# Pair loads from the fifth chunk on, the last ten gate products on VectorE, and a new order in a scan and mixture-of-adapters kernel

## The chip, the cores and the metric

The kernel runs on one core of a Trainium2 chip. A core has five engines with queues of their own: TensorE (PE in the profile; PEld is its loading of weights), VectorE (DVE), ScalarE (ACT), GpSimd (POOL) and SyncE (SP), which here only issues DMAs. The metric is the device time of one execution in microseconds (us), the median of three runs. The profile shows one execution, whose instructions span a little less than its time.

## The reference

Two steps. The first is a linear recurrence along 6400 positions for each of 8 sequences and 128 features; the second sends every row of the result (51200 rows of 128) through two of eight low-rank adapters.

```
h = a[:, t] * h + b[:, t];  x[:, t] = h            # t = 0 .. 6399
logits = x @ w_gate                                # 8 experts
topk = the two largest logits of a row
w = softmax over these two
out = x + sum over the two experts e of w[e] * (x @ A[e]) @ B[e]     # A: 8 x 128 x 16, B: 8 x 16 x 128
```

All arrays are float32. a and b are 26.2 MB each, and so is the output.

## The kernel before, in words

**Tiles.** The 51200 rows are 100 chunks of 512 rows (256 KB of a, of b and of the output). A chunk counts as four blocks of 128 rows. Six blocks make a unit (the last four units have four blocks), four units a group (the last six groups have 2, 2, 1, 1, 1 and 1 units).

**One chunk's way.** SyncE loads a and b (`load`, line 526; the DMA itself is line 541). TensorE transposes them to features by rows (line 562: a to pA, b to pB). ScalarE copies pA to a_st (line 580), VectorE scans (line 613, reading a_st and pB, writing xT in float16; a chunk that holds the border of a sequence is scanned in two pieces). For a unit TensorE multiplies xT with all adapters' A and the gate (line 633, to pZ), and ScalarE copies the result to zl (line 639). For a group the gating (lines 667 to 688) finds the best two experts and their weights g: two maxima and the last product on VectorE, a sigmoid on ScalarE, and the wide steps between on GpSimd, for the last six groups on VectorE instead. Then, again by chunks (`back`, line 693): the gate product zw = zl * g (line 707 on GpSimd, line 711 on VectorE), TensorE transposes zw (line 720), the transposed block is copied to zwT (line 729 on VectorE, line 726 on ScalarE), TensorE adds x and zwT times B in one accumulator (lines 734 and 735), ScalarE copies it to outt (line 744), and SyncE stores it (line 779).

**Loads.** In before the first 8 chunks (HEAD) are loaded singly, 256 KB a DMA, a row of four consecutive rows (2 KB) to each partition, and transposed in four 128-row transposes for a and four for b. From chunk 8 on `paired(c)` (line 523) is true: two chunks come in one DMA of 512 KB, eight consecutive rows (4 KB) to each partition, so that the first chunk of the pair lies in partitions 0 to 63 and the second in 64 to 127. Each takes eight 64-row transposes for a and eight for b. `front` (line 582) interleaves a transpose group of b of chunk c with one of a of chunk c + 1, so that the upper and the lower half of the array work together (line 597): such a group needs the load of b of chunk c and that of a of chunk c + 1, and a step of it feeds the copy of one chunk and the scan of another. Six pairs of buffers hold the loads (12 chunks); a load waits until the transposes of the chunk before it in that buffer are done. Output buffers hold 18 chunks. Stores go in pairs too, except those of the last four chunks.

**Which engine in the tail.** MU_DVE (line 117) lists the chunks, counted from the end, whose gate product is on VectorE: in before 1, 2, 4, 6 and 8, that is chunks 99, 98, 96, 94 and 92. TE_LAST (line 114) lists those of the last 12 chunks whose zwT copy is on ScalarE: none. SPLIT (line 126) sends the stores that begin at chunks 56 and 78 as two DMAs, of 120 and 8 partitions.

**The order.** The program is written as a list of steps, each with an engine, an assumed duration and the steps that it depends on. Before anything runs a planner (`schedule`, line 208) fixes the order on every engine: each step has a rank, its place in a period of six chunks plus TEMPLATE plus NUDGE (line 28), and of the steps whose rank lies within WINDOW of the first in the engine's queue the one that can start earliest goes next. The planner's loads and stores have assumed rates (LOAD_RATE, STORE_RATE, PAIR_RATE). On the chip the engines run these orders and wait for one another by semaphores. `la12` is the load of a that begins at chunk 12, `lb` that of b, `sc` the scan, `A`, `B` and `P` transposes, `te` the zwT copy, `mu` and `md` the gate product on GpSimd and on VectorE.

Of the kernel before, what the change touches and what calls it, by code (L numbers as in the profile page):

```python
# [15 lines left out]
PE_FREE = 0.1  # L16
Q_RATE = {3: 3.6e-3, 5: 2.1e-3, 7: 2.1e-3}
SCAN_SELF = 0.13
ISSUE = {"sp": 0.52, "act": 0.45}
LOAD_RATE = 392e3  # L20
STORE_RATE = 408e3
# [86 lines left out]
START = (-999, "", 0)  # L108
FIRST = -9999
EARLY = -400  # L110
LEAD = []
TAPER = [2, 2, 1, 1, 1, 1]
WIDE_DVE = [1, 2, 3, 4, 5, 6]
TE_LAST = []
TAIL_UNITS = [4, 4, 4, 4]
TE_ACT = [1]
MU_DVE = [1, 2, 4, 6, 8]
TAIL_CHUNKS = 12
WARM0 = 12
WARM = 16  # L120
HALVES = 0.745
PAIR_RATE = 411e3
HEAD = 8
TAIL = 0
STORE_TAIL = [1, 1, 1, 1]
# [754 lines left out]
```

## Time and profile before

| | |
|---|---|
| median of 3 runs | 207.19 us (206.95 to 208.16) |
| the profiled execution | 207.91 us |
| its span, first to last instruction | 205.9 us |
| TensorE clock, mean granted | 0.975 |
| busy: PE, PEld, DVE, ACT, POOL | 184.7, 160.9, 177.7, 169.1, 144.6 us |
| moved by DMA | 79.26 MB, 385 GB/s over the span |
| HBM read, written | 52.56 MB, 26.21 MB |
| VectorE scans (line 613) | 92 whole ones, 1275 ns each |
| gate products on GpSimd (line 707), on VectorE (line 711) | 95 of 1069 ns, 5 of 682 ns |

In the page the span is cut into 40 equal slices; a digit is the busy share of a slice in tenths, PEclk is the clock granted to TensorE, GB/s what the DMA engines moved. In the stretches each engine has its busy microseconds and, in brackets, its instructions, in the order PE, PEld, DVE, ACT, POOL. In a timeline a bracket at the end of a row gives the idle time before it and what ended that. The chain of waits is followed back from the last instruction; its rows are the start and the length of each piece.

### The profile page before, as it was taken

The page shows a single profiled execution, that of the slowest core. Times are in us where ns is not written, and L with a number is a line of the kernel's source. Part 1 is how long each engine was busy: PE and PEld are TensorE (multiplying, and loading weights), DVE is VectorE, ACT ScalarE, POOL GpSimd, SP SyncE. Part 2 cuts the span into 40 slices and gives each one's busy share as a digit, 9 for nine tenths or more (in the row PEclk, how much of TensorE's full clock was granted, in tenths as well). Part 3 has the DMA queues.
Part 4 walks back from the last instruction along what each step waited for, and adds up shares of the span by engine and source line. Part 5 has one row for each costly group of instructions (what it writes and reads, how often), then busy time and mean ns, then how long its engine had stood idle before and what let it go on. Part 6 is the DMA issues. An engine that isn't in the chain of part 4 may idle for free.

```text
span 205.9 us, 7539 instructions
## 1 busy us (share of the span) xinstructions
PE 184.7 (90%) x3152; PEld 160.9 (78%) x3152; DVE 177.7 (86%) x289; ACT 169.1 (82%) x306; POOL 144.6 (70%) x176
## 2 busy tenths in 40 slices
PE   7779589999998899899799999999999999879683
PEld 6557478887897789788689888988888888857572
DVE  0789688998998899798899999999997999989881
ACT  2356668999998999899799999999999998886372
POOL 1000328879898978878788988899989898687420
PEclk9999958999999999999999999999999999999789
DMA  6999999999999999999999999999999999997388
GB/s 191 368 392 415 405 409 406 405 409 405 411 417 406 414 403 417 409 403 416 408 409 400 409 395 408 415 410 411 409 412 410 410 409 404 405 352 289 132 299 300
DMA packets 30559, 79.26 MB, mean 385 GB/s; under 512 B 3774, under 2 KB 3902, under 8 KB 30526
## 3 DMA queue, kind: packets, MB, share of 16 engines
q1 hardware_dynamic: 29054, 78.39, 97.1%
q10 hardware_dynamic: 1472, 0.40, 0.8%
q8 instruction: 25, 0.41, 0.8%
q14 instruction: 8, 0.07, 0.1%
HBM read 52.56 MB, written 26.21 MB: 383 GB/s over the span
## 4 chain that ended last, share of the span: by engine, by line
PE 67%; DVE 12%; DMA 10%; POOL 3%; issue 3%; SPq 2%; ACT 1%; DVEq 0%; POOLq 0%
PE pA L562 14%; PE pB L562 12%; PE pZ L633 11%; PE pO L734 10%; PE pO L720 10%; PE pO L735 9%; DMA a_tm<-in_a_dram 7%; DVE xT L613 5%; DMA b_tm<-in_b_dram 3%; POOL zw L707 3%; SPq L541 2%; DVE zwT L729 2%; DVE zw L711 1%; ACT outt L744 1%; DVE g L688 1%
## 5 line engine op out<-in xcount | busy, mean ns | idle before, releaser
L613 DVE TENSOR_TENSOR_SCAN xT<-a_st,xT,pB 128x512 f16<-128x512 f32 x96 | 120.3, 1253 | 9.5 <-PE pA L562 5.6
L707 POOL TENSOR_TENSOR zw<-zl,g 128x512 f16<-128x512 f32 x95 | 100.4, 1069 | 24.7 <-PE pO L720 11.3
L562 PE MATMUL pB<-ident_f,b_tm 64*128 64x64 f32 (+1 forms) x768 | 71.4, 235 | 6.5 <-DMA a_tm<-in_a_dram 2.8
L580 ACT COPY a_st<-pA 128x512 f32<-128x512 f32 x100 | 60.5, 612 | 17.5 <-PE pA L562 16.0
L562 PE MATMUL pA<-ident_f,a_tm 64*128 64x64 f32 (+1 forms) x768 | 71.7, 235 | 2.0 <-DMA a_tm<-in_a_dram 1.0
L562 PEld LDWEIGHTS pB<-ident_f,b_tm 64*128 64x128 f32 (+1 forms) x768 | 57.9, 142 | 12.5 <-issue 3.7
L562 PEld LDWEIGHTS pA<-ident_f,a_tm 64*128 64x128 f32 (+1 forms) x768 | 57.9, 142 | 8.2 <-DMA a_tm<-in_a_dram 2.3
L639 ACT COPY zl<-pZ 128x816 f32<-128x816 f32 (+1 forms) x68 | 58.0, 853 | 2.3 <-PE pZ L633 1.6
L744 ACT COPY outt<-pO 128x512 f32<-128x512 f32 x92 | 52.7, 609 | 7.7 <-PE pO L735 7.3
L734 PE MATMUL pO<-ident_h,xT 128*128 128x128 f16 x368 | 50.1, 223 | 1.2 <-DVE zwT L729 1.0
L735 PE MATMUL pO<-cst_h,zwT 128*128 128x128 f16 x368 | 48.9, 220 | 0.8 <-issue 0.8
L734 PEld LDWEIGHTS pO<-ident_h,xT 128*128 128x128 f16 x368 | 40.5, 114 | 4.8 <-DVE zwT L729 2.1
L633 PE MATMUL pZ<-cst_h,xT 128*128 128x136 f16 x400 | 36.5, 228 | 1.5 <-DVE xT L613 0.6
L735 PEld LDWEIGHTS pO<-cst_h,zwT 128*128 128x128 f16 x368 | 36.9, 100 | 0.8 <-issue 0.8
L720 PE MATMUL pO<-ident_h,zw 128*128 128x128 f16 x368 | 33.2, 221 | 2.0 <-ACT outt L744 1.3
L729 DVE COPY zwT<-pO 128x512 f16<-128x512 f16 x77 | 30.2, 410 | 3.4 <-PE pO L720 3.1
L633 PEld LDWEIGHTS pZ<-cst_h,xT 128*128 128x128 f16 x400 | 27.1, 115 | 4.4 <-DVE xT L613 1.3
L720 PEld LDWEIGHTS pO<-ident_h,zw 128*128 128x128 f16 x368 | 22.3, 98 | 6.0 <-issue 1.9
L669 POOL TENSOR_TENSOR k<-zl,m 128x192 f32<-128x192 f32 x15 | 7.8, 519 | 22.9 <-DVE m L667 22.9
L671 POOL TENSOR_SCALAR L<-k 128x192 f32<-128x192 f32 x15 | 12.9, 860 | 1.3
L613 DVE TENSOR_TENSOR_SCAN xT<-a_st,pB 128x512 f16<-128x512 f32 (+1 forms) x8 | 7.5, 939 | 4.6 <-PE pB L562 4.3
L678 POOL TENSOR_TENSOR L<-k,m 128x192 f32<-128x192 f32 x15 | 7.9, 524 | 2.8 <-DVE m L676 2.7
(41 smaller groups left out, 106.1 us busy)
## 6 DMA issues: line engine op xcount, KB each, us to landing
a_tm<-in_a_dram SPq DMA_DIRECT2D x46, 512.0 KB, 10.7
b_tm<-in_b_dram SPq DMA_DIRECT2D x46, 512.0 KB, 10.6
out_dram<-outt SPq DMA_DIRECT2D x46, 512.0 KB, 10.8
a_tm<-in_a_dram SPq DMA_DIRECT2D x8, 256.0 KB, 5.8
b_tm<-in_b_dram SPq DMA_DIRECT2D x7, 256.0 KB, 6.0
out_dram<-outt SPq DMA_DIRECT2D x4, 256.0 KB, 2.7
out_dram<-outt SPq DMA_DIRECT2D x2, 480.0 KB
b_tm<-in_b_dram ACTq DMA_DIRECT2D x1, 256.0 KB, 3.6
```

The source lines that it names most:

```text
L562: last = eng["pe"].transpose(*args)
L580: lambda: eng["act"].copy(a_st[c % NA][:, :], pA[:, c % 2, :]), fr(c, "ae"))
L613: last = eng["dve"].tensor_tensor_scan(out=x[:, s0:s1], data0=a_st[c % NA][:, s0:s1], data1=pB[:, c % 2, s0:s1], initial=init, op0=ALU.mul ...
L633: last = eng["pe"].matmul(pZ[:, k // (n // 2), o : o + W], xblock(b0 + k), Awg_h)
L639: return eng["act"].copy(zl[:, zb : zb + n, :].rearrange("p (h k) w -> p h (k w)", h=2), pZ[:, :, 0 : n // 2 * W])
L671: lambda e: e.tensor_scalar(out=ll, in0=kk, scalar1=0.0, scalar2=-1.0e30, op0=ALU.is_ge, op1=ALU.mult), dve=not main)
L707: lambda: eng["pool"].tensor_tensor(out=wv, in0=zv, in1=gv, op=ALU.mult), ba(gi, c, "mu"))
L720: last = eng["pe"].transpose(ptile[:, k * 128 : k * 128 + 128], zw[w][:, k, :], ident_h[:, :])
L729: lambda: eng["dve"].tensor_copy(zwT[w][:, :], ptile[:, 0:C]), ba(gi, c, "te"))
L734: eng["pe"].matmul(dst, xblock(b0 + k), ident_h[:, :], start=True, stop=False)
L735: last = eng["pe"].matmul(dst, zwT[w][:, k * 128 : k * 128 + 128], B_h, start=False, stop=True)
L744: lambda: eng["act"].copy(outt[:, o0 : o0 + n, :].rearrange("p k w -> p (k w)"), bank),
```

## The change

HEAD goes from 8 to 4, so chunks 0 to 3 are loaded singly. FLAT names the pairs 2 to 5, that is chunks 4 to 11: these are loaded two at a time, but in the layout of the single loads (2 KB rows) and with 128-row transposes, and their transposes of a and b are groups of their own. From chunk 12 on everything is as before. MU_DVE takes in all of the last ten chunks, and TE_LAST the zwT copies of chunks 99, 98, 96, 94, 92 and 90. SPLIT is empty. The planner gets two margins (2 us ahead of steps of SyncE, 1 us behind a load), other rates and windows, and new ranks throughout. HEAD_UNITS is empty, so what it touches stays as it was, and the edit to the dependencies of `T` says the same in other words.

```diff
+SP_MARGIN = 2.0
+LAND_MARGIN = 1.0
-LOAD_RATE = 392e3
-STORE_RATE = 408e3
+LOAD_RATE = 387e3
+STORE_RATE = 413e3
 NUDGE = {
...
-    -28.418, "g1_20": 31.602, "g2_15": -5.737, "g2_16": -48.614, "g2_17": -1.558, "g2_18": -9.806, "g2_19": 25.794,
...
+    "A1": 0.12, "A12": -0.295, "A5": -2.998, "B0": 0.543, "B10": 0.408, "B4": -0.719, "B5": -0.252, "B9": 0.072,
...
-WINDOW = {'pe': 16.262, 'act': 17.153, 'dve': 47.02, 'pool': 47.064, 'sp': 57.831}
+WINDOW = {'pe': 8.807, 'act': 27.754, 'dve': 12.829, 'pool': 5.533, 'sp': 45.819}
-TE_LAST = []
+TE_LAST = [1, 2, 4, 6, 8, 10]
+HEAD_UNITS = []
+FLAT = [2, 3, 4, 5]
-MU_DVE = [1, 2, 4, 6, 8]
+MU_DVE = [1, 2, 3, 4, 5, 6, 7, 8, 9, 10]
-PAIR_RATE = 411e3
-HEAD = 8
+PAIR_RATE = 414.5e3
+HEAD = 4
-SPLIT = {56: [120, 8], 78: [120, 8]}
+SPLIT = {}
 TEMPLATE = {
-    "la": [-13.284, -13.376, -10.147],
-    "lb": [-12.856, -11.393, -13.112],
-    "A": [3.619, 4.619, -4.264, 6.619, 7.619, 8.619],
-    "B": [-2.245, 2.718, -8.407, 8.99, 6.061, 4.41],
+    "la": [-6.553, -4.617, -2.553],
+    "lb": [-6.553, -4.553, -2.553],
+    "A": [0.912, 2.517, 3.517, 4.517, -3.092, 9.66],
+    "B": [-0.301, 3.648, 4.517, 1.944, 6.315, 7.517],
...
+    def margin(self, d, op):
+        return (SP_MARGIN if op.eng == "sp" else 0.0) + (LAND_MARGIN if d.sem is not None else 0.0)
...
-                users[d.i].append((op, self.lag(d, op)))
+                users[d.i].append((op, self.lag(d, op) + self.margin(d, op)))
...
         def paired(c):
-            return HEAD <= c < NCH - TAIL
+            return HEAD <= c < NCH - TAIL and c // HC not in FLAT
...
-                    q, f"{key}{c}", n * C * D * 4 / (PAIR_RATE if paired(c) else LOAD_RATE),
+                    q, f"{key}{c}", n * C * D * 4 / (PAIR_RATE if paired(c) else STORE_RATE if n == HC else LOAD_RATE),
```

More of the change, by code (lines that the diff above doesn't have):

```diff
@@ L121 @@
 HALVES = 0.745
-PAIR_RATE = 411e3
-HEAD = 8
+PAIR_RATE = 414.5e3
+HEAD = 4
 TAIL = 0
 STORE_TAIL = [1, 1, 1, 1]
-SPLIT = {56: [120, 8], 78: [120, 8]}
+SPLIT = {}
 TEMPLATE = {
-    "la": [-13.284, -13.376, -10.147],
-    "lb": [-12.856, -11.393, -13.112],
-    "A": [3.619, 4.619, -4.264, 6.619, 7.619, 8.619],
-    "B": [-2.245, 2.718, -8.407, 8.99, 6.061, 4.41],
-    "ae": [-1.493, 12.357, 10.831, 7.96, 5.931, 11.772],
-    "sc": [-2.149, -1.286, 6.521, -19.69, -9.638, -0.216],
-    "Z": [6.623, 2.916, -2.696, 9.959],
-    "ze": [6.413, 12.686, 18.636, 4.611],
-    "g1": [1.078],
-    "g2": [15.192],
-    "g3": [12.311],
-    "g4": [-7.624],
-    "g5": [43.586],
-    "g6": [18.91],
-    "w1": [27.261],
+    "la": [-6.553, -4.617, -2.553],
+    "lb": [-6.553, -4.553, -2.553],
+    "A": [0.912, 2.517, 3.517, 4.517, -3.092, 9.66],
+    "B": [-0.301, 3.648, 4.517, 1.944, 6.315, 7.517],
+    "ae": [-6.291, 2.578, 3.093, 6.695, 6.06, 7.06],
+    "sc": [-1.377, -1.34, 1.899, 2.384, 4.614, 4.743],
+    "Z": [-1.773, 4.921, 1.502, 2.727],
+    "ze": [-4.588, 0.759, -5.543, 3.442],
+    "g1": [3.016],
+    "g2": [4.586],
+    "g3": [3.551],
+    "g4": [2.992],
+    "g5": [3.066],
+    "g6": [1.968],
+    "w1": [3.121],
     "w2": [27.183],
@@ L146 @@
     "p3": [35.473],
-    "mu": [22.377, 11.789, 38.051, -6.995, 25.901, 25.822],
-    "T": [17.564, 18.694, 15.643, 19.013, 20.568, 20.925],
-    "te": [11.47, 21.167, 12.791, -1.785, 1.996, 11.732],
-    "D": [13.525, 17.402, 15.169, 14.035, 19.652, 27.901],
-    "oe": [26.926, 32.894, 33.316, 36.556, 35.829, 26.06],
-    "st": [25.679, 26.621, 29.881],
-    "ta": [14.725, 30.746, 16.943, 18.052, 19.161, 20.27],
-    "md": [78.718, -0.018, -87.87, 12.1, 13.209, 14.318],
+    "mu": [11.649, 11.861, 13.38, 13.442, 14.624, 15.545],
+    "T": [11.704, 10.769, 11.92, 12.841, 15.097, 14.896],
+    "te": [11.106, 11.632, 13.124, 14.809, 14.966, 15.856],
+    "D": [10.274, 11.213, 12.116, 13.037, 15.506, 24.201],
+    "oe": [2.576, 7.213, 7.951, 8.765, 12.054, 10.102],
+    "st": [27.605, 29.678, 31.678],
+    "ta": [-10.83, 12.148, -0.969, 14.045, 14.966, 15.887],
+    "md": [10.94, 11.861, 13.636, 13.703, 14.624, 15.545],
     "wu": [-0.198],
-    "ch": [26.813],
+    "ch": [2.449],
     "mb": [0.0],
-    "q2": [17.668],
-    "q3": [-16.399],
-    "q5": [-0.842],
-    "q6": [-2.93],
-    "q7": [1.928],
+    "q2": [4.085],
+    "q3": [3.453],
+    "q5": [3.066],
+    "q6": [3.093],
+    "q7": [3.107],
     "q8": [35.473],
-    "g7": [47.426],
-    "g8": [9.111],
+    "g7": [3.107],
+    "g8": [3.132],
 }
@@ L348, in bass_associative_scan_2x2__then__mixture_of_adapters_kernel @@
     b0 = 0
-    for n in [U] * ((NBLK - sum(TAIL_UNITS)) // U) + TAIL_UNITS:
+    for n in HEAD_UNITS + [U] * ((NBLK - sum(HEAD_UNITS) - sum(TAIL_UNITS)) // U) + TAIL_UNITS:
         units.append((b0, n))
@@ L513, in un @@
         def un(u, kind):
-            return (PERIOD * (u // GMAX), kind, u % GMAX)
+            v = u - len(HEAD_UNITS)
+            if v < 0:
+                return ((units[u][0] + units[u][1] - 1) // J - 1, kind, 0)
+            return (sum(HEAD_UNITS) // J + PERIOD * (v // GMAX), kind, v % GMAX)
         def ga(gi, kind):
@@ L721, in tr @@
                 return last
-            o_T[c] = P.add("pe", f"T{c}", 0.1 + 0.056 * n, [(o_mu[c], True), (o_ih, True)] + free + [(o, True) for o in o_wu if c < 2], tr, ba(gi, c, "T"))
+            o_T[c] = P.add("pe", f"T{c}", 0.1 + 0.056 * n, [(o_mu[c], True), (o_ih, True)] + free + [(o, True) for o in (o_wu if c < 2 else [])], tr, ba(gi, c, "T"))
             if te_act(c):
```

95 rows, old and new, of the table NUDGE are left out of this document.

## The prediction

> **What bounds the kernel now.** I read the slices first, then busy time by stretches, then the chain of waits and the timelines of the first 30 and the last 25 us. The page's span and slices:
>
> ```profile
> span 205.9 us, 7539 instructions
> ...
> PEclk9999958999999999999999999999999999999789
> DMA  6999999999999999999999999999999999997388
> GB/s 191 368 392 415 405 409 406 405 409 405 411 417 406 414 403 417 409 403 416 408 409 400 409 395 408 415 410 411 409 412 410 410 409 404 405 352 289 132 299 300
> DMA packets 30559, 79.26 MB, mean 385 GB/s; under 512 B 3774, under 2 KB 3902, under 8 KB 30526
> ```
>
> A slice is 205.9 / 40 = 5.15 us. From the third to the 35th the DMA engines are full at about 409 GB/s; only the first two slices and the last five fall short. The bytes do not change, so time can be won only where they are short: 79.26 MB at 409 GB/s is 193.8 us, and the other 12.1 us lie at the ends. Busy time by stretches (engine, busy us, count; then granted clock, DMA share, GB/s):
>
> ```profile
> 0.00:10.00 10.00, 7.28 (x40) 6.11 (x41) 3.56 (x5) 3.25 (x5) 0.70 (x6) 1.00 0.84 276
> ...
> 24.00:40.00 16.00, 15.12 (x256) 13.02 (x256) 13.64 (x18) 13.07 (x22) 10.92 (x14) 0.79 1.03 409
> 40.00:180.00 140.00, 134.14 (x2508) 118.63 (x2504) 130.43 (x198) 130.04 (x236) 121.29 (x146) 1.00 1.03 409
> 180.00:206.00 26.00, 17.98 (x238) 15.01 (x235) 18.87 (x62) 14.47 (x31) 11.09 (x10) 0.93 0.74 274
> ```
>
> The first 10 us move 2.76 MB where 409 GB/s would give 4.09: 3.3 us lost. The last 26 us run at 274: (409 - 274) / 409 x 26 = 8.6 us lost. That is the 12 us. In the last stretch only stores are left and they wait for results: the compute chain, with VectorE (third pair of numbers) its fullest engine, sets the end. In the body VectorE is busy 130.43 of 140 us. Who waits for whom, SyncE's queue and then VectorE in the body (40 to 175 us):
>
> ```profile
> SPq L541 <- PE pA L562: 40.9, 25, 4.5
> ```
> ```profile
> DVE xT L613 <- PE pA L562: 3.8, 8, 1.1
> ```
>
> Loads wait 40.9 us for TensorE to free their buffers, so in the body compute is behind the loads. An idle microsecond saved on VectorE anywhere is a microsecond off the end, until the DMA floor: 193.8 + 3.3 + 2.2 for the last store (the final output copy of the chain below ends at 203.05; 205.9 - 203.05 = 2.85, of which 256 KB at 409 take 0.64) = 199.3 us of span. So at most 6.6 us can be won.
>
> **Head: four single loads, then pairs with 2 KB rows.** The VectorE, TensorE and SyncE rows of the head (start, length, what, idle before and releaser):
>
> ```profile
> 11.26 2.67 DVE L613 TENSOR_TENSOR_SCAN xT<-a_st,xT,pB 128x512 f16<-128x512 f32 x2 [0.61 <-ACT a_st L580]
> ...
> 14.08 6.89 DVE L613 TENSOR_TENSOR_SCAN xT<-a_st,xT,pB 128x512 f16<-128x512 f32 x5 [0.15 <-PE pB L562]
> 21.15 1.28 DVE L613 TENSOR_TENSOR_SCAN xT<-a_st,xT,pB 128x512 f16<-128x512 f32 x1 [0.18 <-PE pB L562]
> ...
> 24.64 2.12 DVE L613 TENSOR_TENSOR_SCAN xT<-a_st,xT,pB 128x512 f16<-128x512 f32 x2 [1.44 <-PE pA L562]
> ```
> ```profile
> 23.89 0.27 PE L562 MATMUL pB<-ident_f,b_tm 64*128 64x64 f32 x1 [1.95 <-DMA a_tm<-in_a_dram]
> ```
> ```profile
> 12.42 0.33 SPq L541
> ...
> 12.79 13.62 DMA a_tm<-in_a_dram
> 26.41 0.04 issue
> 26.46 0.36 PE pB L562
> ```
>
> Counted from the start, 11.26 is the scan of chunks 3 and 4, 14.08 of 5 to 9, 21.15 of 10, 24.64 of 11 and half of 12.
> - *Later.* Chunk 4 now lands with chunk 5: 0.52 MB / 409 GB/s = 1.28 us later. Its scan cannot start at 12.6 but near 14.08, and the row of five that follows without a wait moves with it: +1.3 us up to chunk 10, which ends at 23.6 instead of 22.43.
> - *Earlier.* In before, B of chunk 11 is one instruction group with A of chunk 12 and waits for that load: TensorE sits 1.95 us at 23.89 and the scan of chunk 11 begins at 24.64. Flat chunks have transposes of their own, and b of chunk 11 lands in one load with b of 10, which the scan at 21.15 already reads. Chunk 11 then starts at 23.6: 1.0 us earlier.
> - *Order of loads.* One load is issued at 12.42, the next at 12.79 lands 13.62 us later, and chunk 13 starts on it; the ranks of before (14 to 16 with -31.994 on la16) put a of chunk 16 ahead of a of 14. In the new ranks la14 stands at 12 - 4.617 = 7.4 and la16 at 12 - 2.553 = 9.4, so the wait for chunk 14 should shrink by one load, again 1.28 us. I take -1.2 for the whole head; bounds +1.3 (the first item alone) and -2.3 (second and third).
> - *128-row transposes* for chunks 8 to 11. Eight 128-row ones take 8 x 0.11 = 0.89 us, sixteen paired 64-row ones 0.65 us (both rows below, the second from 33.55 to 34.20). 4 x 0.24 = 1.0 us more TensorE time, beside scans of 1.28 us a chunk that hide it; uncovered it costs that 1.0.
>
> ```profile
> 11.52 0.89 PE pA L562 x8
> ...
> 33.55 0.21 PE pB L562
> ...
> 34.20 0.01 PE pA L562
> ```
>
> - *Issues.* One issue holds the SyncE queue for:
>
> ```profile
> 7.97 0.43 SPq L541 DMA_DIRECT2D b_tm<-in_b_dram  x1
> ```
>
> Sixteen single issues become eight, plus four of pairs: 4 x 0.43 us less on the SyncE queue, and the loads of chunks 8 on come off it sooner. At nothing: the DMA engines are already full. If the singles held slices 2 and 3 down, up to (1 - 368/409) x 5.15 + (1 - 392/409) x 5.15 = 0.7 us comes back; 2 KB rows for chunks 8 to 11 at 392 instead of 409 cost 0.2.
> - *Whole stores* of chunks 56 and 78 (before: 120 + 8 rows): two issues of 0.43 us go, hidden by the same full queue; 0 to -0.9.
>
> **Tail: gate products and copies.** The chain of the last 23 us, and GpSimd and TensorE beside it:
>
> ```profile
> 189.37 0.60 DVE zw L711
> 189.97 1.07 DVE k L680 x2
> 191.04 0.60 DVE zw L711
> 191.64 0.96 DVE g L688
> 192.60 0.34 DVE zwT L729
> ...
> 193.41 0.11 PE pO L734
> ...
> 196.82 0.06 PE pO L734
> ...
> 198.83 0.23 DVE k L680 x2
> ...
> 199.39 0.20 DVE g L688 x2
> ...
> 201.88 1.17 ACT outt L744 x2
> ```
> ```profile
> 189.90 2.65 POOL L707 TENSOR_TENSOR zw<-zl,g 128x512 f16<-128x512 f32 x2 [0.91 <-PE pA L720]
> ```
> ```profile
> 191.70 0.40 PE L720 MATMUL pB<-ident_h,zw 128*128 128x128 f16 x4 [1.21 <-DVE zw L711]
> ```
>
> - *Adds.* Products of chunks 90, 91, 93, 95 and 97 come to VectorE: 5 x 0.60 = +3.0 us.
> - *Removes.* The copies zwT of chunks 90, 92, 94, 96, 98 and 99 go to ScalarE: 6 x 0.34 = -2.0 us. ScalarE takes six at its own rate,
>
> ```profile
> L726 ACT COPY zwT<-pO 128x512 f16<-128x512 f16 x15 | 9.2, 614 | 0.4 <-PE pO L720 0.4
> ```
>
>   3.7 us in all, of the 26 - 14.47 = 11.5 us that it is idle there: hidden but for the last, 0.614 against VectorE's 0.34, so 0.2 to 0.3 us longer in the chain (0.2 taken).
> - *Collision gone.* While GpSimd multiplies from 189.90 to 192.55, two VectorE instructions on line 680 take 1.07 us and one on 688 takes 0.96; without GpSimd the pairs take 0.23 and 0.20. That is 0.84 + 0.86 = -1.7 us.
> - *Clock.* After that stretch TensorE, which waited 1.21 us on the product, runs at 0.11 us a step from 193.41 to 196.82 instead of 0.06. These 3.4 us would be 3.4 x 0.06 / 0.11 = 1.9 at full clock: 1.5 us. If the gaps close, this goes; if not, nothing. I take -1.0, two thirds, since the wait hangs on the two VectorE instructions that get short.
> Tail: 3.0 - 2.0 + 0.2 - 1.7 - 1.0 = -1.5 us; bounds +1.2 (neither collision nor clock helps) and -2.0.
>
> **Ranks.** Planner only: its wait times gain 2 us for SyncE and 1 us behind a load, so it places such work later. The price is idle VectorE in the body, which no row of before shows for the new order. The nearest rows are its own best and worst stretches:
>
> ```profile
> 40.00:60.00 20.00, 19.26 (x368) 17.15 (x365) 19.47 (x28) 19.35 (x36) 17.12 (x23) 1.00 1.03 407
> 60.00:90.00 30.00, 27.68 (x524) 24.49 (x521) 26.96 (x39) 26.78 (x49) 26.17 (x32) 1.00 1.03 411
> ```
>
> The body has 9.6 us idle. At the rate of the first row (0.53 in 20) it would be 3.7: -5.9 us. At the second (3.04 in 30) 14.2: +4.6 us. I take 0, the mean of the body as it is, and keep both ends.
>
> **Sum.** -1.2 - 1.5 = -2.7 us of span: 203.2. The profiled execution took 207.91 us, 2.0 beyond its span, and lay 0.72 over the median of 207.19. Against the median: **204.5 us**, 1.3% faster; with small misses on both sides 202.5 to 206.
>
> **Rivals.**
> - *The gains are covered.* Chunk 4's delay eats the head (0 instead of -1.2), and the tail keeps only what is sure (3.0 - 2.0 + 0.2 - 1.7 = -0.5). For it: VectorE's work in the tail grows by 1.0 us. Against: the 1.95 us wait has one cause, and it goes. 206.7 to 207.2, no measurable change.
> - *The floor is reached.* The order improves the body as well, and DMA stays full to the end: 207.19 - 6.6 = 200.6. For it: 9.6 us idle in the body. Against: VectorE is at 97% only in the best 20 us.
> - *The order loses.* The margins hold transposes back and the scans wait as from 60 to 90 us all the way: -2.7 + 4.6 = +1.9, 209.1. For it: that stretch exists. Against: loads land long before use there.
> - *A cold clock in the head* (the other side). Pair loads give TensorE longer waits between 8 and 20 us. Before has the pattern: behind the 1.95 us wait at 23.89 the stretch from 24 to 40 us got a clock of 0.79, so 0.21 x 16 = 3.4 us of TensorE time. Once more, ten microseconds earlier, plus chunk 4's 1.3 us, with the tail's -1.5: +3.2, 210.4. It decides where a wait near 2 us comes between two bursts; from 5 to 20 us before has none of that length, the longest being:
>
> ```profile
> 9.52 0.66 PE L562 MATMUL pB<-ident_f,b_tm 128*128 128x128 f32 x4 [0.70 <-DMA b_tm<-in_b_dram]
> ```
>
>   [...]
>
> **How the numbers follow.** About 1% (2.1 us) is what this kernel's measurement can tell from no change: faster is below 205.1, slower above 209.3. Chances: forecast 0.42, floor 0.10, covered 0.24, order loses 0.14, cold head 0.10. Faster: nine tenths of the forecast and the floor, 0.48. Slower: the cold head and seven tenths of the losing order, whose price of 209.1 lies at the edge, 0.20. Same: 0.32. The range takes the floor below (200.6) and the cold head above (210.4).
>
> **What would show it.** In the profile after: one scan of chunk 4 beginning near 14 us and chunk 11 by 23.6 without a wait on the a load; the a load of 14 issued before that of 16; no GpSimd product in the last ten chunks and lines 680 and 688 short throughout; a clock of 9 in the last three slices; VectorE idle in the body near 9.6 us. The prediction is wrong if that last number moves by more than 3 us, since the ranks are the one term that no row prices, or if TensorE turns cold before 20 us.

## The result and the profile after

The changed kernel takes 204.38 us (median of four runs, 204.18 to 204.83), the kernel before beside it on the same chip 207.07 us (206.02 to 208.16). The ratio is 0.987 with a 95% interval of 0.9835 to 0.9906: 1.3% faster. The profiled execution took 204.18 us, with a span of 202.4 us against 205.9, so 3.5 us less. About 1 us of that is spread between executions: the medians differ by 2.7 us, but the profiled execution of before lay 0.84 us over its median and that of after 0.20 us under its own. Ratios are taken over the executions in the fast state, so they can differ a little from the quotient of two medians.

The page of the kernel after, its span and slices (one slice is now 5.06 us):

```profile
span 202.4 us, 7466 instructions
...
PEclk9999999999999999999999999999999999999999
DMA  6999999999999999999999999999999999999994
GB/s 187 366 387 391 408 409 407 403 413 406 410 414 410 408 412 416 410 411 407 414 408 413 411 407 410 419 406 411 410 416 408 410 410 414 405 402 371 342 354 153
```

The hole at 132 GB/s near the end is gone, and so are both dips of the clock (slices 6 and 7, and 38 and 39). The first three slices are as short as they were, the fourth is a little shorter (391 instead of 415). What remains below 400 GB/s is the first 20 us and the last 20.

Busy time by stretches of the kernel after (the columns are those of the prediction: PE, PEld, DVE, ACT, POOL with their instructions, then granted clock, DMA share and GB/s):

```profile
0.00:24.00 24.00, 19.84 (x157) 17.35 (x157) 14.83 (x15) 13.17 (x21) 2.73 (x10) 1.00 0.97 344
24.00:40.00 16.00, 14.04 (x268) 12.03 (x267) 14.82 (x21) 13.68 (x25) 12.95 (x16) 1.00 1.03 406
40.00:180.00 140.00, 133.21 (x2498) 117.57 (x2495) 129.43 (x197) 130.43 (x237) 120.27 (x145) 1.00 1.03 410
180.00:203.00 23.00, 14.59 (x207) 11.73 (x205) 15.35 (x58) 14.80 (x33) 2.08 (x2) 0.97 0.81 306
```

VectorE has done 29.65 us of work by 40 us, where before had done 28.44: it is 1.2 us ahead. From 40 to 180 us it is idle for 10.6 us instead of 9.6, and gives 1.0 us of that back. So by VectorE's busy time the two kernels stand nearly level at 180 us, and the gain lies behind that point. There VectorE has 15.35 us of work left (before: 18.87), although five more gate products are among it. Part of the reason is the copies zwT (line 729 of before, 682 of after), VectorE's busy time and their number behind 180 us:

```profile
180.00:206.00 26.00, 7.27 (x18) 0.93 0.74 274
```
```profile
180.00:203.00 23.00, 3.69 (x9) 0.97 0.81 306
```

Nine are gone, 3.6 us. Six of them went to ScalarE by TE_LAST; the other three were done before 180 us, which is the new order. The other part is what VectorE's rows by form show, first before, then after; lines 680 and 688 of before are 633 and 641 of after:

```profile
L688 DVE SCALAR_TENSOR_TENSOR g<-L,sd 128x32 f32<-128x32 f32 x4 | 1.5, 399 | 0.5 <-ACT sd L682 0.5
L680 DVE TENSOR_TENSOR k<-k,L 128x32 f32<-128x32 f32 x4 | 1.4, 403 | 0.0
L688 DVE SCALAR_TENSOR_TENSOR g<-L,sd 128x96 f32<-128x96 f32 x2 | 1.2, 609 | 0.0
```
```profile
L664 DVE TENSOR_TENSOR zw<-zl,g 128x512 f16<-128x512 f32 x10 | 6.8, 677 | 0.0
...
L633 DVE TENSOR_TENSOR k<-k,L 128x32 f32<-128x32 f32 x4 | 0.7, 181 | 0.0
...
L641 DVE SCALAR_TENSOR_TENSOR g<-L,sd 128x32 f32<-128x32 f32 x4 | 0.7, 178 | 0.0
...
L641 DVE SCALAR_TENSOR_TENSOR g<-L,sd 128x96 f32<-128x96 f32 x2 | 0.5, 241 | 0.0
```

Four instructions with a mean of 399 ns now have 178, four of 403 have 181, two of 609 have 241: 0.88 + 0.89 + 0.74 = 2.5 us less for the same work. VectorE also no longer idles there. It ends at 195.39 us instead of 201.73; from 180 us to those ends it was idle for 201.73 - 180 - 18.87 = 2.9 us before and for 0.04 us after.

Equal busy time at 180 us also hides a difference of order. The last scan begins at 185.34 us in before and at 181.49 in after, 3.9 us earlier, and the output copies run 4 us ahead there (the 81st ends at 180.69 and at 176.72 us). In the stretch ahead of that (from 167 us to the last scan but one) VectorE does 34 instructions in before and 25 in after: copies and gating steps that before puts ahead of the last scans stand behind them in after.

The last output copy, on ScalarE's timeline, ends at 197.90 us where before ended at 203.05:

```profile
197.32 0.58 ACT L697 COPY outt<-pB 128x512 f32<-128x512 f32 x1 [0.24 <-PE pB L688]
```

So the computation ends 5.15 us earlier, but the span only 3.5. From the last copy to the end of the span it was 2.85 us, and it is 4.5: 1.65 us are given back while the last stores drain. In stretches of 5 us the end looks like this:

```profile
185.00:190.00 5.00, 4.12 (x62) 3.32 (x59) 5.00 (x21) 4.18 (x10) 0.00 (x0) 1.00 0.84 320
190.00:195.00 5.00, 4.31 (x63) 3.56 (x64) 5.00 (x22) 4.15 (x11) 0.00 (x0) 1.00 0.95 359
195.00:200.00 5.00, 1.92 (x28) 1.44 (x26) 0.39 (x1) 2.58 (x5) 0.00 (x0) 1.00 0.85 312
```

VectorE is busy for all of 185 to 195 us and the clock is full; the DMA share is 0.84 to 0.95. VectorE and the stores now set the end together. What the drain is made of is told at the end of the section on the prediction.

The tally of the span is then: head -1.2, body +1.0, tail about -5.0 (5.15 less the 0.2 by which VectorE leads at 180 us), drain +1.65, together -3.5.

### The profile page after: what moved, and what is told of

Its sections match the earlier page's. It is cut to its first block, busy times and chain, and to the rows that moved or that the text cites. A ratio compares the mean times of both kernels' runs of the same rounds, so it can differ in the third digit from the quotient of the medians.

```text
span 202.4 us, 7466 instructions
## 1 busy us (share of the span) xinstructions
PE 181.7 (90%) x3120; PEld 158.7 (78%) x3120; DVE 174.4 (86%) x288; ACT 172.1 (85%) x312; POOL 138.0 (68%) x171
## 4 chain that ended last, share of the span: by engine, by line
PE 54%; DVE 22%; DMA 13%; ACT 3%; issue 3%; POOL 2%; DVEq 0%; POOLq 0%
DMA a_tm<-in_a_dram 13%; DVE xT L566 12%; PE pA L515 11%; PE pB L515 10%; PE pO L673 8%; PE pO L687 8%; PE pZ L586 8%; PE pO L688 6%; DVE zwT L682 3%; DVE zw L664 3%; DVE g L641 2%; POOL zw L660 2%; PE pO L433 1%; ACT outt L697 1%; ACT a_st L533 1%
## 5 line engine op out<-in xcount | busy, mean ns | idle before, releaser
L660 POOL TENSOR_TENSOR zw<-zl,g 128x512 f16<-128x512 f32 x90 | 95.1, 1061 | 20.5 <-DVE g L641 17.0
L515 PE MATMUL pA<-ident_f,a_tm 64*128 64x64 f32 (+1 forms) x752 | 70.3, 233 | 1.3 <-issue 1.0
L515 PEld LDWEIGHTS pB<-ident_f,b_tm 64*128 64x128 f32 (+1 forms) x752 | 56.1, 139 | 10.1 <-DMA b_tm<-in_b_dram 2.0
L592 ACT COPY zl<-pZ 128x816 f32<-128x816 f32 (+1 forms) x68 | 57.0, 838 | 6.6 <-PE pZ L586 5.7
L515 PEld LDWEIGHTS pA<-ident_f,a_tm 64*128 64x128 f32 (+1 forms) x752 | 56.5, 139 | 6.5 <-issue 0.9
L697 ACT COPY outt<-pO 128x512 f32<-128x512 f32 x92 | 54.3, 601 | 1.7 <-PE pO L688 1.6
L687 PE MATMUL pO<-ident_h,xT 128*128 128x128 f16 x368 | 51.2, 222 | 2.4 <-DVE zwT L682 2.0
L688 PE MATMUL pO<-cst_h,zwT 128*128 128x128 f16 x368 | 50.2, 219 | 0.5 <-issue 0.5
L673 PE MATMUL pO<-ident_h,zw 128*128 128x128 f16 x368 | 35.4, 220 | 2.5 <-POOL zw L660 1.4
L679 ACT COPY zwT<-pO 128x512 f16<-128x512 f16 x16 | 9.5, 591 | 0.5 <-PE pO L673 0.5
```

Source lines behind the costliest of these rows:

```text
L515: last = eng["pe"].transpose(*args)
L592: return eng["act"].copy(zl[:, zb : zb + n, :].rearrange("p (h k) w -> p h (k w)", h=2), pZ[:, :, 0 : n // 2 * W])
L660: lambda: eng["pool"].tensor_tensor(out=wv, in0=zv, in1=gv, op=ALU.mult), ba(gi, c, "mu"))
L673: last = eng["pe"].transpose(ptile[:, k * 128 : k * 128 + 128], zw[w][:, k, :], ident_h[:, :])
L687: eng["pe"].matmul(dst, xblock(b0 + k), ident_h[:, :], start=True, stop=False)
L688: last = eng["pe"].matmul(dst, zwT[w][:, k * 128 : k * 128 + 128], B_h, start=False, stop=True)
```

## The experiments

The question is whether the change is a sum of parts (an earlier head, and a tail without collisions between VectorE and GpSimd), as the prediction has it, or whether the gain comes from the new order and the parts bring little by themselves. What each theory expected of a run stands in the quoted text. The first six kernels took one part away, or put one in, and let the planner make its order anew from the ranks given to it. The next five write the planner's final order out as lists of step names, one for each engine, and make one edit in them; nothing else moves then. The last takes the computation away.

### Parts through the planner

**ranks_only** is the new ranks, margins and windows with the head and the lists of before:

```diff
-FLAT = [2, 3, 4, 5]
+FLAT = []
-HEAD = 4
+HEAD = 8
-MU_DVE = [1, 2, 3, 4, 5, 6, 7, 8, 9, 10]
+MU_DVE = [1, 2, 4, 6, 8]
-TE_LAST = [1, 2, 4, 6, 8, 10]
+TE_LAST = []
-SPLIT = {}
+SPLIT = {56: [120, 8], 78: [120, 8]}
```

> The kernel after with the head, the two engine lists and the split stores of before: only margins, rates, windows and ranks are new. By the prediction's sum (ranks 0, head -1.2, tail -1.5) it takes the time of before, 206.5 to 207.6 us, and GpSimd's products again lengthen VectorE's instructions on the gating lines in the last 20 us. If the new order carries the gain, 205.5 or less, with the last VectorE instruction ending clearly before 201.7 us.

Measured: 210.68 us, ratio 1.015 (1.0115 to 1.0186), slower than before. VectorE's timeline in the head:

```profile
23.22 2.60 DVE L566 TENSOR_TENSOR_SCAN xT<-a_st,xT,pB 128x512 f16<-128x512 f32 x2 [5.17 <-PE pB L515]
```

The scan sits idle for 5.2 us in front of chunks 8 and 9, longer than any wait that either of the two kernels has there.

**new_no_head** undoes the head alone:

```diff
-FLAT = [2, 3, 4, 5]
+FLAT = []
-HEAD = 4
+HEAD = 8
```

> The kernel after with the head of before (eight single loads, then 4 KB pairs with 64-row transposes). By the prediction 205.6 us (204.4 + 1.2), with TensorE waiting near 2 us before chunk 11. If the head is covered by the stores that drain at the end: 204.2 to 204.7, no change, and the VectorE work ends later all the same.

Measured: 210.41 us, ratio 1.0106 (1.0033 to 1.0179). It has the same wait:

```profile
23.43 2.60 DVE L566 TENSOR_TENSOR_SCAN xT<-a_st,xT,pB 128x512 f16<-128x512 f32 x2 [5.34 <-PE pB L515]
```

With eight single loads the new ranks put the cast of the constants behind the eighth chunk's scan on VectorE (17.81 us). TensorE's first products with the adapters need it, and VectorE's next scan then waits 5.34 us for the transposes of the first pair. This measures a bad order, not the worth of the head.

**old_ranks_head** is before with only the new head (and the planner's rate for such loads):

```diff
+FLAT = [2, 3, 4, 5]
-HEAD = 8
+HEAD = 4
...
```

> The kernel before, its ranks kept, with four single loads and flat pairs for chunks 4 to 11. By the prediction 205.9 us (-1.2): chunk 4's scan moves 1.3 us later, chunk 11's no longer waits for the a load of chunk 12. But la16 still stands ahead of la14 in these ranks, so if that order was what counted, chunk 13 still starts near 27.6 us and the time stays at 206.8 to 207.5. If the old ranks do not fit the new steps, above 208.

Measured: 222.63 us, ratio 1.0744 (1.0711 to 1.0778). A row of its waits (in total, times, longest):

```profile
DVE xT L614 <- ACT a_st L581: 9.0, 3, 8.1
```

The scan waits 8.1 us at a stretch, and VectorE does 8.05 us of work in the first 24 us instead of the 14.80 of before.

**old_ranks_tail** is before with only the two lists of the tail:

```diff
-TE_LAST = []
+TE_LAST = [1, 2, 4, 6, 8, 10]
-MU_DVE = [1, 2, 4, 6, 8]
+MU_DVE = [1, 2, 3, 4, 5, 6, 7, 8, 9, 10]
```

> The kernel before, its ranks kept, with all ten last gate products on VectorE and six zwT copies on ScalarE. By the prediction 205.6 us (-1.5): lines 680 and 688 short again, TensorE at full clock to the end. If only the new order makes use of it: 206.7 to 207.5, or later where old ranks place the moved steps badly.

Measured: 308.35 us, ratio 1.4859 (1.477 to 1.4948). The steps that change engine carry other names, and for some of these names before's tables hold ranks that were never used at that place. They land far from where they belong and hold up every engine; the largest of its waits:

```profile
DVE zwT L729 <- PE pO L720: 60.5, 32, 9.0
```

**tail_in_old_order** takes that fault away: the moved steps keep the names, and with them the ranks, that they had before.

```diff
+MU_PLACE = [3, 5, 7, 9, 10]
-                    "dve", f"md{c}", 0.142 + 0.133 * n, deps,
+                    "dve", (f"mu{c}" if NCH - c in MU_PLACE else f"md{c}"), 0.142 + 0.133 * n, deps,
...
```

> The kernel before with the ten gate products on VectorE and six zwT copies on ScalarE, each moved step keeping the rank of the step it replaces, so that body and head keep their order. By the prediction's tail (-1.5): 205.6 us, with lines 680 and 688 near 0.2 us a pair and the last VectorE instruction about 1.5 us earlier than 201.7. If the lists give nothing without the new ranks: 206.7 to 207.5 with the last VectorE instruction at 201.5 to 202.5.

Measured: 233.4 us, ratio 1.1265 (1.1219 to 1.1312). From 180 to 200 us:

```profile
180.00:200.00 20.00, 13.65 (x125) 11.05 (x126) 11.70 (x35) 9.01 (x18) 5.33 (x5) 0.50 0.32 108
```

It is 75 us faster than the kernel with the strange ranks, and still 12.6% slower than before. A step on another engine gets another queue and another time in the plan, and the planner seems to rearrange the tail around it; that is argued and not shown step by step. The stores fall to 108 GB/s and TensorE runs at half its clock throughout.

**new_order_no_tail** is the reverse, the kernel after without its lists, with ranks handed down in the same way:

```diff
-TE_LAST = [1, 2, 4, 6, 8, 10]
+TE_LAST = []
-MU_DVE = [1, 2, 3, 4, 5, 6, 7, 8, 9, 10]
+MU_DVE = [1, 2, 4, 6, 8]
...
```

> The kernel after with the lists of before (five products back on GpSimd, the six copies back on VectorE), each step keeping its place in rank. By the prediction 205.9 us (204.4 + 1.5), collisions back. If the end of after is already set by the drain of stores, VectorE ends later by 1.5 us but the time stays within 0.5 of 204.4.

Measured: 237.83 us, ratio 1.1478 (1.1425 to 1.1531), with a clock of 0.59 from 180 to 200 us.

What follows from the six: ranks fit only the set of steps for which they were made. Each of these kernels is between 1% and 49% slower than before, and all parts together gain 1.3%. So these runs cannot price a part; for that the order has to stay still.

### One edit in a written-out order

**old_load_order** is the kernel after with six names of SyncE's list put into the order of before:

```diff
-la12 lb12 la14 lb14 la16 lb16
+lb12 la12 la16 la14 lb14 lb16
```

> The kernel after with its order on every engine written out, and one change: the loads from chunk 12 on issued as in before (b of 12, a of 12, a of 16, a of 14, b of 14, b of 16). By the prediction's third head item the scan of chunk 13 starts one load (1.28 us) later than its 27.16 us, and the time is 205.7. If a head delay is made up before the end, chunk 13 is late but the time is 204.2 to 204.7.

Measured: 204.61 us, ratio 0.9881 (0.9843 to 0.9918), the same as the kernel after. VectorE's timeline of after (chunk 11 with half of 12, then 13), then that of this kernel:

```profile
24.26 2.16 DVE L566 TENSOR_TENSOR_SCAN xT<-a_st,xT,pB 128x512 f16<-128x512 f32 x2 [0.40 <-ACT a_st L533]
...
27.16 1.27 DVE L566 TENSOR_TENSOR_SCAN xT<-a_st,xT,pB 128x512 f16<-128x512 f32 x1
```
```profile
25.40 2.16 DVE L642 TENSOR_TENSOR_SCAN xT<-a_st,xT,pB 128x512 f16<-128x512 f32 x2 [1.68 <-ACT a_st L609]
...
28.30 1.27 DVE L642 TENSOR_TENSOR_SCAN xT<-a_st,xT,pB 128x512 f16<-128x512 f32 x1
```

The order of six loads alone moves chunks 11 and 13 by 1.14 us (1.28 us against chunk 10, which begins 0.14 us earlier here). That is nearly the whole lead of 1.2 us that after has over before at 40 us. The delay stays to the end of the computation:

```profile
198.48 0.58 ACT L773 COPY outt<-pB 128x512 f32<-128x512 f32 x1 [0.24 <-PE pB L764]
```

The last copy ends at 199.06 us instead of 197.90, and yet the span is 202.2 us against 202.4. The drain behind it is 3.1 us instead of 4.5. This profiled execution is the fastest of six, whose spans lie between 202.2 and 204.0 us with a median of 202.4. An earlier head of 1.14 us is therefore worth nothing that shows in the time of this kernel: the drain takes it back.

**singles_to_7** is the kernel after with chunks 4 to 7 loaded one at a time again, each load in SyncE's list right behind that of its pair:

```diff
-load(c, 1 if c < HEAD else HC)
+load(c, 1 if c < 8 else HC)
```

> The kernel after, orders written out, with chunks 4 to 7 loaded singly (a4 b4 a5 b5 ...), all else the same. By the prediction's first head item chunk 4 could start 1.3 us earlier (13.80 to 12.6) and the time falls to 203.1. If TensorE's order (A4 A5 Z0 before B4) or the drain at the end covers it, 204.2 to 204.7.

Measured: 204.27 us, ratio 0.9859 (0.9829 to 0.9889), not to be told from the kernel after. Chunk 4 in VectorE's timeline, in after and then here:

```profile
13.80 6.93 DVE L566 TENSOR_TENSOR_SCAN xT<-a_st,xT,pB 128x512 f16<-128x512 f32 x5 [1.15 <-PE pB L515]
```
```profile
13.52 6.93 DVE L642 TENSOR_TENSOR_SCAN xT<-a_st,xT,pB 128x512 f16<-128x512 f32 x5 [1.15 <-PE pB L591]
```

Chunk 4 alone in its load starts 0.28 us earlier, not 1.3, and even this is not its load: the very first scan begins 0.29 us earlier in this execution (6.71 instead of 7.00 us). Chunk 4 waits 1.15 us for TensorE's transpose in both. In the new order TensorE does A of chunks 4 and 5 and the first product with the adapters before B of chunk 4, and that product waits 0.76 us in after for the cast of the constants, which VectorE begins at 12.38 us behind the scan of chunk 3. The size of the load does not set the start of chunk 4.

**before_with_lists** is the kernel before with its own order, in which only five products go from GpSimd's list to VectorE's and six copies from VectorE's to ScalarE's, each at the place where its inputs are ready (the places were chosen by hand):

```diff
-TE_LAST = []
+TE_LAST = [1, 2, 4, 6, 8, 10]
-MU_DVE = [1, 2, 4, 6, 8]
+MU_DVE = [1, 2, 3, 4, 5, 6, 7, 8, 9, 10]
```

> The kernel before with its order written out and only the two lists changed: the products of chunks 90, 91, 93, 95 and 97 stand on VectorE, each beside the product that followed it, and the six zwT copies on ScalarE, each ahead of the next output copy; nothing else moves. By the prediction's tail 205.7 us (207.2 - 1.5), the two VectorE pairs on lines 680 and 688 short and TensorE not cold from 193 us. If the lists are worth nothing by themselves: 206.8 to 207.6.

Measured: 207.47 us, ratio 1.0007 (0.9989 to 1.0025): no change. VectorE's last instruction ends at 199.51 us, 2.2 us earlier than in before, so the lists do in the old order what they were counted for. Two rows show where it goes, ScalarE's timeline and one stretch:

```profile
199.40 1.19 ACT L802 COPY zwT<-pB 128x512 f16<-128x512 f16 x2
200.71 1.19 ACT L820 COPY outt<-pB 128x512 f32<-128x512 f32 x2
```
```profile
192.00:195.00 3.00, 2.03 (x36) 2.03 (x37) 2.06 (x8) 2.20 (x6) 0.00 (x0) 1.00 0.06 23
```

The copies of the last two chunks line up on ScalarE, four of 0.6 us one behind another, and the last ends at 201.90 us, 1.15 earlier than in before. The last scan begins at 185.17 us, as late as in before. And the stores still have their hole from 192 to 195 us, at 23 GB/s, with no product on GpSimd and the clock at full. So neither of these makes the hole. In the old order ScalarE makes no output copy from 191.40 to 193.65 us, and the stores behind that come in one burst. The drain grows to 3.6 us.

**new_order_old_lists** is the kernel after with its order, in which both lists are undone by hand.

```diff
-TE_LAST = [1, 2, 4, 6, 8, 10]
+TE_LAST = []
-MU_DVE = [1, 2, 3, 4, 5, 6, 7, 8, 9, 10]
+MU_DVE = [1, 2, 4, 6, 8]
```

> The kernel after with its order written out and both lists undone: the five products at the end of GpSimd's queue, the six copies on VectorE beside their neighbours. By the prediction's tail 205.9 us (204.4 + 1.5). As the run with the old order of loads showed an end 1.1 us later in compute and no later in time, the drain of stores may cover about 1 us: 204.9. If the new order alone carries the gain: 204.2 to 204.7.

Measured: 206.7 us, ratio 0.9972 (0.9949 to 0.9996). The new order and the new head without the lists are worth 0.3%, and the lists on top of them the rest: 0.987 against 0.9972 is 1.0%, some 2.1 us. GpSimd's timeline, then VectorE's, then TensorE's:

```profile
184.74 1.07 POOL L736 TENSOR_TENSOR zw<-zl,g 128x512 f16<-128x512 f32 x1
188.72 2.08 POOL L736 TENSOR_TENSOR zw<-zl,g 128x512 f16<-128x512 f32 x2 [2.91 <-DVE L L703]
```
```profile
184.82 1.04 DVE L703 TENSOR_TENSOR L<-L,k 128x32 f32<-128x32 f32 x1
...
188.96 0.87 DVE L717 SCALAR_TENSOR_TENSOR g<-L,sd 128x32 f32<-128x32 f32 x1
189.75 0.17 DVE L705 TENSOR_REDUCE m<-L 128x4 f32<-128x32 f32 x1
189.85 0.41 DVE L758 COPY zwT<-pA 128x512 f16<-128x512 f16 x1
190.18 0.67 DVE L707 TENSOR_TENSOR L<-k,m 128x32 f32<-128x32 f32 x1
```
```profile
186.25 0.29 PE L763 MATMUL pO<-ident_h,xT 128*128 128x128 f16 x1 [1.52 <-DVE zwT L758]
```
```profile
183.00:186.00 3.00, 1.59 (x20) 1.10 (x20) 2.97 (x9) 1.80 (x5) 2.09 (x2) 0.99 0.99 382
186.00:189.00 3.00, 2.75 (x26) 2.67 (x27) 2.07 (x12) 0.71 (x2) 0.28 (x1) 0.50 0.69 264
```

The chain can be read off these rows. Small instructions that take 0.18 us in after take 1.04, 0.87 and 0.67 here, and each ends where a product of GpSimd ends: at 184.82 + 1.04 = 185.86 against 184.74 + 1.07 = 185.81, at 189.83 against 189.76 for the first of the two from 188.72 (half of 2.08), at 190.85 against 190.80 for the second. The copy behind the first one comes late, TensorE stands idle for 1.52 us, and in the next 3 us its clock is at 0.50. VectorE ends at 200.31 us, 4.9 later than in after. But the last scan begins at 181.51 us, as early as in after: the 3.9 us by which it comes sooner belong to the order and not to the lists.

**new_order_no_products** puts only the five products back on GpSimd, and leaves the copies on ScalarE:

```diff
-MU_DVE = [1, 2, 3, 4, 5, 6, 7, 8, 9, 10]
+MU_DVE = [1, 2, 4, 6, 8]
```

> The kernel after with its order written out and only the five products put back on GpSimd. By the prediction's terms VectorE loses 3.0 us of products and gains 1.7 of collisions, so its last instruction is up to 1.3 us earlier than 195.4 unless the chain waits for GpSimd; with the drain at the end 203.5 to 204.5. If collisions and a cold TensorE cost more than the products, above 204.9.

Measured: 205.81 us, ratio 0.9942 (0.9908 to 0.9975). So the products are worth 0.7%, about 1.5 us, and the copies 0.3%; the second lies within the intervals. The profiled execution is the fastest of eight, 1.0 us under their median. The last stretch of this kernel:

```profile
180.00:206.00 26.00, 14.33 (x207) 11.67 (x204) 16.61 (x53) 14.73 (x33) 7.53 (x7) 0.95 0.71 269
```

VectorE has five products of 0.68 us less to do than in after, 3.4 us, and is busy for 16.61 us, 1.3 us more. Five instructions have again 0.67 to 1.05 us. Work taken from VectorE lengthens what stays on it, as long as it goes to GpSimd.

### The transfers alone

**dma_alone** has the loads and stores of after in the same order, without any computation between them. A load waits only for the load that held its buffer before, and the stores send a constant.

```diff
-                for key, v in waits[op.i]:
-                    handle.wait_ge(s_eng[key] if key in s_eng else s_dma[key], v)
-                inst = op.emit()
+                if op.sem is None:
+                    continue
...
+                op.emit().then_inc(s_dma[op.sem], 16)
```

> The kernel after's loads and stores in its order on SyncE, with all compute left out: a load waits only for the load before it in its buffer, stores wait for one fill of the output buffer, so the output is a constant. By the prediction's floor a span of 199.3 us (201.3 in time), stores by themselves at the same 409 GB/s as the mixed body. If stores alone move slower than the mix (after moves 320 to 359 GB/s at the end), the last 20 stores show it at under 380 GB/s and the floor is higher, 200 to 202 of span: then after is at it.

Measured: 198.3 us (198.03 to 198.39), a span of 196.6 us. By stretches (here DVE, POOL, clock, DMA share, GB/s):

```profile
0.00:10.00 10.00, 5.18 (x1) 2.86 (x5) 1.00 0.88 276
...
24.00:160.00 136.00, 0.00 (x0) 0.00 (x0) 1.00 1.03 414
...
180.00:190.00 10.00, 0.00 (x0) 0.00 (x0) 1.00 1.05 407
```

The slow first 10 us belong to the transfers themselves: 276 GB/s here, 275 in after. The body runs at 414 GB/s, not 409, and stores alone at 407. So the floor of this order of transfers is 196.6 us of span, and after stands 5.8 us above it. Its 410 GB/s from 40 to 180 us cost it 140 x 4 / 414 = 1.4 us, and the rest, 4.4 us, is lost behind 180 us, above all where its stores run at 312 to 359 GB/s from 185 to 200 us.

## Why the prediction was right, and where it was not

The time was 204.38 us against 204.5; by the medians 2.7 us were won, as the sum had it. That the sum came out is in part luck. In time, the runs give the head next to nothing instead of -1.2 (old_load_order, singles_to_7), the new order with the new head some -0.6 instead of 0 for the ranks (new_order_old_lists), and the lists some -2.1 instead of -1.5.

- *What bounds the kernel.* That an idle microsecond of VectorE counts held in the body and, in the tail, up to the last result. It did not hold to the end of the span: 5.15 us of computation became 3.5 (the drain), and the 1.14 us of old_load_order became nothing. The step that failed is the 2.85 us behind the last copy, taken as fixed (2.2 and the 0.64 of a transfer). It is 2.5 to 4.5 us in the kernels with written-out orders, before and after.
- *The floor.* 199.3 was taken, 196.6 measured. The rate of 409 GB/s was read from a kernel whose loads wait 40.9 us for buffers; the transfers by themselves do 414.
- *Head, -1.2.* The number is not the sum of its items: +1.3, -1.0 and -1.28 give -1.0, and as chunk 11 at 23.6 already stands behind the late chunk 10, the prediction's own times give -2.3. It was a choice between the bounds. Its size is right at 40 us (28.44 to 29.65 us of work), the items are not. *Later*: chunk 4 was set near 14.08 us and begins at 13.80; chunk 10 was to end at 23.6 and does (22.34 + 1.28). But singles_to_7 shows that the landing of the pair is not the cause; TensorE's order is. *Earlier*: chunk 11 was to begin at 23.6 without a wait for the a load of 12. It begins at 24.26. Its transposes are a group of their own, as forecast, but the new order puts A of chunk 12 ahead of them, and TensorE's timeline of after shows the wait:

```profile
22.87 0.71 PE L515 MATMUL pA<-ident_f,a_tm 64*128 64x64 f32 x8 [0.27 <-DMA a_tm<-in_a_dram]
23.51 0.66 PE L515 MATMUL pB<-ident_f,b_tm 128*128 128x128 f32 x4
```

  *Order of loads*: right and the largest item. It was priced at one load, 1.28 us, and the six names measure 1.14; to the a load of 14, ahead of that of 16 as forecast, comes that of 12, now ahead of b of 12, which the forecast had missed. Together with the drain the head's part of the final time is about nothing.
- *Ranks, 0.* Right in the body: idle time went from 9.6 to 10.6 us, within the 3 us named. But "planner only" missed what the order does in the tail: it brings the last scan 3.9 us forward and three copies out of the tail. With the lists alone the slowest 3 us of the stores before 198 us run at 23 GB/s, with the new order alone (new_order_old_lists) at 154, with both none below 333.
- *Tail, -1.5.* The kind of each term is right: a product on VectorE takes 0.68 us and holds it for 0.60 of them until the next instruction begins, as taken; collisions go, the clock stays up. Two sizes are off. The collisions were counted on three instructions, -1.7; the groups give -2.5. The gaps and the clock were taken at -1.0; VectorE's idle time in the tail fell by 2.9. The computation of the tail ends about 5.0 us earlier, and the drain takes 1.65 back. Part of the 5.0 us is the order's and not the lists'. In time the lists are worth some 2.1 us in the new order and nothing in the old one, so a single price for them did not exist.
- *Whole stores* were never tried by themselves.

The rivals. The *cold clock in the head* did not come in this kernel: the granted clock is 1.00 in every stretch up to 180 us. It did come in new_no_head, where the granted clock is 0.90 in the first 24 us and 0.72 from 24 to 40 us. The *losing order* did not come for this set of steps; ranks_only and new_no_head show what it looks like, a wait of 5.2 us in the head. The *floor* was not reached. *The gains are covered* was half right: it named chunk 4 as the cover of the head, and the drain behind the last copy is the cover.

**What the drain is made of.** The last four single stores take 4.4 us (median) from issue to landing in after, 3.0 in old_load_order and 2.7 in before. The traces of before and after show part of the reason. They have 16 landings for each of these stores, which fits the 16 DMA engines. Of the last store of after 14 come between 200.42 and 200.58 us, the other two at 201.27 and 201.91: by that reading two engines run behind. In before all 16 lie between 205.08 and 205.37 us. From the middle landing to the last it is 1.4 us in after and 0.2 in before; this is 1.2 of the 1.65 us. Less this lag the drain is 3.1 us in after and 2.6 in before.

The lag goes with transfers that the page of after lists as a queue of their own, by its name those that load the program itself:

```profile
q8 instruction: 25, 0.41, 0.8%
```

Each is 16 KB and takes 0.9 to 1.2 us. In after the lag is 4.0 us at 189 us, and the last of these transfers falls at 197.61 us, into the drain; the second latest landing goes there from 0.3 to 1.9 us behind the middle one. In before the lag was 3.5 us at 187 us, but from 192 to 195 us the DMA engines moved 26 GB/s, and behind that hole it is 0.2; the last of these transfers falls at 197.19 us, and of the next store to land the last landing is 0.9 us behind. So in after, whose stores have no such hole, the lag lasts to the end. That these transfers cause it is the author's reading: the traces show that they come together in time. The rest is covered by the issue of the last store, which holds SyncE for 0.98 us in after and 0.33 in before; why is not shown.

One thing stays open: the worth of the new head as such, since every kernel with the old head got another order as well.

## What to carry to other kernels

In a program whose order is made by a list of ranks, price an edit in the finished order, and move one step by hand; planned anew, kernels with parts of a 1.3% gain were 1% to 49% slower. Where instructions of one engine grow longer beside another's work, as VectorE's did here from 0.18 to as much as 1.04 us beside GpSimd's products, count every one of them by its row, and set against it what it takes alone: here that made five added instructions of 0.68 us a gain. And follow a gain to the last transfer: what lies behind the last result is not a constant (2.5 to 4.5 us here), and two late landings of the last store's 16 went with 1.2 us of it.

## What the runs showed of the hardware

**Which instructions collide.** In new_order_old_lists two products of GpSimd run from 188.72 to 190.80 us. In that time VectorE's reduction and its copy out of pA take 0.17 and 0.41 us, as in after (170 and 412 ns). The two instructions with two inputs in SBUF, g from L and sd and L from k and m, take 0.87 and 0.67 us, against 178 and 177 ns in after, and end with the products: at 189.83 against 189.76 us, and at 190.85 against 190.80.

**How much idle time stood ahead of a half clock.** In the trace of before the granted clock stays at one value for 20.48, 6.83, 160.43 and 3.41 us, whole multiples of 3.41 us. Cut into pieces along these changes, before shows the piece ahead of its first fall to 0.50, the piece ahead of the second with the cold one behind it, and a late piece behind which the clock stays up; the piece of after is of that last kind:

```profile
22.62:26.03 3.41, 1.68 (x38) 1.45 (x38) 1.65 (x3) 1.58 (x4) 1.98 (x3) 1.00 1.03 412
189.87:193.29 3.42, 1.53 (x25) 1.19 (x22) 3.42 (x9) 1.02 (x3) 2.65 (x2) 1.00 0.50 190
193.29:196.70 3.41, 3.41 (x36) 3.41 (x34) 1.79 (x6) 2.27 (x5) 0.16 (x1) 0.50 0.40 149
200.11:203.53 3.42, 1.95 (x24) 1.38 (x24) 1.47 (x4) 1.83 (x4) 0.00 (x0) 1.00 1.04 384
```
```profile
194.90:198.31 3.41, 2.02 (x28) 1.54 (x28) 0.48 (x1) 2.68 (x5) 0.00 (x0) 1.00 0.97 357
```

TensorE is busy for 1.68 and 1.53 us of the pieces ahead of the two falls, whose longest waits end at 23.89 us (1.95 us) and at 191.70 us (1.21 us), and for 1.95 and 2.02 us of the two behind which the clock stays at 1.00. In new_order_old_lists the clock goes from 0.99 to 0.50 with a wait of 1.52 us (the stretches of 3 us in its own paragraph). So in before TensorE was idle for 1.73 and 1.88 us of a piece of 3.41 us ahead of a fall, in waits no longer than 1.95 us. Where a limit lies is not shown by so few pieces.
